# A kernel ordered by tables of planned times: retuned tables, tables of their own for the first steps, two key buffers, and first query loads issued by ScalarE

## The chip, the cores and the metric

The kernel runs on one core of a Trainium2 chip. The metric is the device time of one execution in microseconds. Before the change it is 1298.58 us, the median of three runs (1295.53 to 1300.79). The profiled execution has a span of 1298.1 us and a mean granted TensorE clock of 0.963. The engines are PE (TensorE, with PEld for its weight loads), DVE (VectorE), ACT (ScalarE), POOL (GpSimd) and SP (SyncE, which here only issues transfers).

## The reference

```python
# q, k, v: 8 batches, 8 heads, 576 rows, 64 columns, float32
scores = np.matmul(q, k.transpose(0, 1, 3, 2)) / np.sqrt(64)
kth = np.partition(scores, -32, axis=-1)[..., -32:-31]   # 32nd largest of each row
scores = np.where(scores >= kth, scores, -1e9)
attn = softmax(scores)                                    # over the kept entries
x = (attn @ v) regrouped as (4608 tokens, 512)
h = x @ w_in                                              # 512 x 1024
solu = h * softmax(h)
ln = (solu - mean(solu)) / sqrt(var(solu) + 1e-6) * g_ln
return ln @ w_out                                         # 1024 x 512
```

The weights arrive as 64-bit numbers and are turned into float32 on the chip, in 16 chunks of 128 by 512 (8 of `w_in`, 8 of `w_out`).

## The kernel before, in words

All the work is in `fast_path`. After it one number, `bad`, tells whether some row was not handled by the fast method; only then a general path would run, and with these inputs it does not.

**The attention is cut into 32 steps**, four for each of the eight batches. A step handles nine query tiles of 128 rows against 576 keys: two head pairs, two chunks of 128 rows of each head, and one tile that gathers the last 64 rows of two heads. For a step `i` the functions run as follows; the letter is the engine.

- Keys: `load_k` (SP, L653 to L665, one 256 KB transfer and two small ones for the last 64 rows of queries and keys), `load_v` (L667), `prep_t` and `prep_k` (PE transposes, L695 and L708), `prep_tc` and `prep_kc` (ACT copies, L701 and L718), `moments` (PE, L729) and `moments_c` (ACT, L735). There is one head pair's worth of these per step.
- Queries: `load_q` (SP, L739 to L751: four transfers of 64 KB and two of 16 KB), `prep_q` (PE transposes), `prep_qc` (ACT copy to `qT`, L769).
- A first guess of each row's threshold: `spread` (PE, `y_ps` L780), `spread_v` (DVE, `yq` L798), `spread_r` (DVE, L809), `first_p` (POOL, square root and scaling, L814 to L820), `first` (DVE, L828).
- Scores: `scores` (PE, `s_ps` L858, two tiles at a time) and `evac` (ACT, copy to `X`, L867, one for each of nine tiles).
- Thresholds made better by counting: `count0` (DVE, L875), `second` (DVE, L886), `count1` (seven by ACT, L897, and two by DVE, L875), `third` (DVE, L909), `count2` (ACT, `sg` L932), `side` (DVE, `al` L941). Then `nearest` and `best` (DVE, L953 and L960) find the eight scores nearest to the threshold, and `count_off` (ACT) and `kth` (DVE) choose the exact 32nd largest among them.
- Softmax: `exps` (ACT, L968), `keep` (DVE, mask and sum, L997), `inverse` (DVE, L1005), `norm` (POOL, L1012).
- Output: `transpose_p` (PE, `tp_p` L1026) and `copy_p` (ACT, `PT` L1038), `transpose_last` (PE, L1056) and `copy_last` (ACT, L1064) for the last 64 columns, `attn_v` (PE, `om` L1075) and `copy_v` (ACT, `xTm` L1087), each once for either head pair.

**The second block is cut into 36 token tiles** of 128 tokens. A tile runs through `mm1` (PE, `h_ps` L1099, two halves of four matmuls each), `hexp` (ACT), `solu` (DVE), `square` (ACT), `ln` (POOL), `transpose_ln` (PE) and `copy_ln` (ACT), `mm2` (PE, `o_ps` L1157, two halves) and `store` (ACT copy to `osb` L1164 and a transfer). Its first matmul reads `xTm`, which two steps together fill: so tile `t` of batch `b` is placed two steps after that batch's step `t`.

**The weight chunks**: `load_w` (SP), `w_bits` (DVE, `w_tmp`, L589 to L597), `w_low` (ACT, L605), `w_mul` and `w_add` (POOL), `w_gain` (POOL). At the end each chunk is loaded once more and its range tested: `w_again`, `w_exp`, `w_check`.

**The order is written out by hand.** Every call of such a function gets a planned time from a table; the list of calls is sorted by it and emitted in that order, and this fixes the queue of instructions of PE, ACT, DVE and POOL. An engine takes its queue strictly in order and waits where an operand is not ready. The transfers that SP issues follow in the order of their calls.

```python
    for i in range(NSTEP):
        all_times(i * STEP, step_times, i)
    for n in range(len(pairs)):
        for f, times in key_times:
            at(n // NP * NP * STEP + times[n % NP], f, n)
...
    with tc.manual_schedule(engines={E.PE, E.Activation, E.DVE, E.Pool}):
        for _, _, f, args in sorted(todo, key=lambda x: x[:2]):
            f(*args)
```

`STEP` is 39, and times are only places in the order. `step_times` holds one place for each call of a step and is the same for all 32 steps; `key_times` has four places for each call, one for each head pair of a batch; `first_times` serves the token tiles of batch 0, `token_times` the later ones, `tails_times` and `last_times` the tiles of left-over rows and those after the last step; `weights_times` has absolute places.

**Buffers** come from pools: `p1` has one buffer for each name, `p2` two, `p4` four, `p8` eight. `km`, the keys as loaded, is in `p1`: the next `load_k` waits until PE has read the last one in `prep_k` and `moments`. `qm` is in `p1` too. In PSUM there are three pools of two buffers each: `ps_big` for scores, `y_ps` and `h_ps`; `ps_tp` for transposes; `ps_o` for `om`, `o_ps` and `pre`, the product of `prep_t` and `moments`.

Of the kernel before, what the change touches and what calls it, by code (L numbers as in the profile page):

```python
# [15 lines left out]
P = 128  # L16
# [427 lines left out]
def fast_path(  # L444
# [23 lines left out]

    nc = tc.nc
# [30 lines left out]

    pairs = [(b, hp) for b in range(B) for hp in range(NP)]
    steps = []
    for b in range(B):
        for half in range(2):
            for n in range(NP // 2):
                two = (2 * n + half, 2 * n + 1 - half)
                chunks = [(hp, 2 * half + t) for hp in two for t in range(2)]
                steps.append((b, chunks, two[0]))
# [144 lines left out]
    def load_k(n):  # L653
# [4 lines left out]
        d["k"] = p1.tile([P, 2 * NM, D], F32, tag="km", name="km")  # L658
# [80 lines left out]
    def load_q(i):  # L739
        b, chunks, x = steps[i]  # L740
        d = st[i]
        d["q"] = p1.tile([P, NT, D], F32, tag="qm", name="qm")
        for c, (hp, t) in enumerate(chunks):
            nc.sync.dma_start(
# [5 lines left out]
        for h in range(2):  # L750
            nc.sync.dma_start(  # L751
                out=d["q"][h * ST : (h + 1) * ST, 2 * NM, :], in_=q[b, 2 * x + h, SM:S, :]
            )

    def keys_of(i, c):

        b, chunks, x = steps[i]
        return ks[NP * b + (x if c == NM else chunks[c][0])]
# [217 lines left out]
    def kth(i):  # L976
# [3 lines left out]
        hot = small.tile([P, NT, 8], F32, tag="hot", name="hot")  # L980
# [84 lines left out]

    def attn_v(i, part):
        o = st[i]["om", part] = ps_o.tile([P, 512], F32, tag="o", name="om")
        n = 2 * P if part else SP
        vm, vt = keys_of(i, 2 * part)["v"]
        pt = pt_of(i, part)[:, :, 0:n]  # L1070

        for c in range(NM + 1):
            for h in range(2):
                hd = slice(h * ST, (h + 1) * ST)
                nc.tensor.matmul(  # L1075
                    out=o[h * D : (h + 1) * D, 0:n],
                    lhsT=vm[:, h, c, :] if c < NM else vt[hd, :],
                    rhs=pt[:, h * NM + c, :] if c < NM else pt[hd, 2 * NM, :],
                    start=(c == 0), stop=(c == NM),
                )  # L1080

    def copy_v(i, part):
        b, chunks, x = steps[i]
        hp, t = chunks[2 * part]
        o = st[i]["om", part]
        m = once(xs, ("m", b, t // 2), lambda: p2.tile([P, NP, 2 * P], F32, tag="xTm", name="xTm"))
# [256 lines left out]
    for f, needed, chunks, times in weights_times:  # L1343
        for n, time in zip(chunks, times):
            if needed:
                at(time, f, n)
# [105 lines left out]
```

## Time and profile before

| what | value |
|---|---|
| time, median of three runs | 1298.58 us (1295.53 to 1300.79) |
| profiled span | 1298.1 us |
| PE busy | 1194.8 us, 92%, 6243 matmuls |
| DVE busy | 1154.8 us, 89%, 2974 instructions |
| ACT busy | 1118.8 us, 86%, 2446 instructions |
| POOL busy | 479.6 us, 37%, 583 instructions |
| costliest group of PE | `o_ps` L1157, 576 matmuls, 261.8 us |
| costliest group of DVE | `junkv` L875, 288 counts of 801 ns, 230.7 us |
| costliest group of ACT | `sg` L932, 256 counts of 768 ns, 195.6 us |
| bytes moved | 57.00 MB, mean 44 GB/s |

Three engines are busy for most of the time, so the sums over the whole span do not say which of them holds up the end: that has to be read stage by stage. The profile has a view for this, which gives each engine's busy time in chosen stretches, and one that lists, for each engine, which instruction of it waited for which instruction of another, how long in all, how often, and how long at most. A third one follows the chain of work that ended last back to the start and adds up its parts by engine.

### The profile page before, as it was taken

The page shows a single profiled execution, that of the slowest core. Times are in us where ns is not written, and L with a number is a line of the kernel's source. Part 1 is how long each engine was busy: PE and PEld are TensorE (multiplying, and loading weights), DVE is VectorE, ACT ScalarE, POOL GpSimd, SP SyncE. Part 2 cuts the span into 40 slices and gives each one's busy share as a digit, 9 for nine tenths or more (in the row PEclk, how much of TensorE's full clock was granted, in tenths as well). Part 3 has the DMA queues.
Part 4 walks back from the last instruction along what each step waited for, and adds up shares of the span by engine and source line. Part 5 has one row for each costly group of instructions (what it writes and reads, how often), then busy time and mean ns, then how long its engine had stood idle before and what let it go on. Part 6 is the DMA issues. An engine that isn't in the chain of part 4 may idle for free.

```text
span 1298.1 us, 20306 instructions
## 1 busy us (share of the span) xinstructions
PE 1194.8 (92%) x6243; PEld 658.0 (51%) x6243; DVE 1154.8 (89%) x2974; ACT 1118.8 (86%) x2446; POOL 479.6 (37%) x583
## 2 busy tenths in 40 slices
PE   5645879999999999999999999999999999998996
PEld 3323445555555555555555555555555555554543
DVE  4899999999999997999999997999999997999612
ACT  3787889999999889999999889999999889999534
POOL 4244654443333234443333244443333234443310
PEclk9666889999999999999999999999999999999999
DMA  6212211101110111101210112111210111102421
GB/s 163 81 43 61 67 38 28 37 22 37 46 36 17 30 32 50 34 23 31 54 36 18 30 30 54 28 29 30 55 35 19 31 28 43 30 9 73 130 73 44
DMA packets 106246, 57.00 MB, mean 44 GB/s; under 512 B 89224, under 2 KB 97424, under 8 KB 106128
## 3 DMA queue, kind: packets, MB, share of 16 engines
q1 hardware_dynamic: 106128, 55.61, 15.7%
q8 instruction: 52, 0.85, 0.3%
q14 instruction: 66, 0.54, 0.1%
HBM read 46.14 MB, written 9.44 MB: 43 GB/s over the span
## 4 chain that ended last, share of the span: by engine, by line
PE 59%; ACT 18%; DVE 15%; issue 3%; POOL 3%; DMA 1%; SPq 0%; DVEq 0%; POOLq 0%; ACTq 0%
PE o_ps L1157 15%; PE s_ps L858 12%; PE h_ps L1099 12%; PE tp_p L1026 7%; PE om L1075 7%; DVE junkv L875 4%; ACT junka L897 4%; DVE E L997 3%; ACT sg L932 3%; ACT PT L1038 2%; PE tp_ln L1146 2%; ACT E L968 2%; DVE w L953 2%; DVE w L960 2%; ACT X L867 2%
## 5 line engine op out<-in xcount | busy, mean ns | idle before, releaser
L1157 PE MATMUL o_ps<-w_out,lnT 128*128 128x512 f32 x576 | 261.8, 598 | 0.2 <-ACT osb L1164 0.2
L875 DVE TENSOR_SCALAR_CACHE_REDUCE junkv<-X,t 128x576 bf16<-128x576 f32 x288 | 230.7, 801 | 11.9 <-ACT X L867 7.3
L1012 POOL TENSOR_SCALAR E<-E,rden 128x576 f32<-128x576 f32 x256 | 204.7, 813 | 87.0 <-DVE rden L1008 76.5
L925 POOL TENSOR_SCALAR tt<-t 128x9 f32<-128x9 f32 x32 | 21.8, 680 | 573.3 <-DVE t L919 573.3
L1099 PE MATMUL h_ps<-w_in,xTm 128*128 128x512 f32 x512 | 226.7, 595 | 0.3 <-ACT xTm L1087 0.3
L953 DVE SCALAR_TENSOR_TENSOR w<-X,al,sg 128x576 f32<-128x576 f32 x256 | 210.6, 824 | 0.1
L960 DVE MAX8 w<-w 128x8 f32<-128x576 f32 x288 | 210.5, 749 | 0.0
L997 DVE SCALAR_TENSOR_TENSOR E<-X,kth,E 128x576 f32<-128x576 f32 x256 | 200.0, 818 | 9.7 <-ACT E L968 9.6
L858 PE MATMUL s_ps<-kT,qT 64*128 64x288 f32 x1024 | 195.7, 458 | 5.5 <-ACT X L867 4.5
L932 ACT ACTIVATE sg<-X,t 128x576 bf16<-128x576 f32 x256 | 195.6, 768 | 2.8 <-DVE t L919 2.8
L897 ACT ACTIVATE junka<-X,t 128x576 bf16<-128x576 f32 x224 | 174.3, 778 | 19.4 <-DVE t L888 15.6
L867 ACT ACTIVATE X<-s_ps 128x576 f32<-128x576 f32 x256 | 157.2, 655 | 36.0 <-PE s_ps L858 32.4
L1026 PE MATMUL tp_p<-ident,E 128*128 128x128 f32 x1024 | 155.5, 285 | 26.4 <-POOL E L1012 21.6
L1026 PEld LDWEIGHTS tp_p<-ident,E 128*128 128x128 f32 x1024 | 116.0, 144 | 92.9 <-issue 37.5
L1038 ACT COPY PT<-tp_p 128x512 f32<-128x512 f32 x256 | 145.6, 595 | 19.5 <-PE tp_p L1026 19.3
L1157 PEld LDWEIGHTS o_ps<-w_out,lnT 128*128 128x128 f32 x576 | 104.3, 190 | 110.6 <-issue 107.8
L1099 PEld LDWEIGHTS h_ps<-w_in,xTm 128*128 128x128 f32 x512 | 94.6, 190 | 109.7 <-issue 102.4
L968 ACT ACTIVATE E<-X 128x1152 f32<-128x1152 f32 x128 | 146.5, 1174 | 0.0
L1075 PE MATMUL om<-PT,vm 128*64 128x256 f32 (+1 forms) x1024 | 140.0, 416 | 0.0
L858 PEld LDWEIGHTS s_ps<-kT,qT 64*128 64x128 f32 x1024 | 116.2, 199 | 46.7 <-ACT X L867 18.1
L1075 PEld LDWEIGHTS om<-PT,vm 128*64 128x64 f32 x1024 | 68.5, 138 | 59.7 <-issue 22.5
L818 POOL TENSOR_TENSOR zs<-zs,phalf 128x9 f32<-128x9 f32 x32 | 70.2, 2194 | 2.7
(127 smaller groups left out, 1631.8 us busy)
## 6 DMA issues: line engine op xcount, KB each, us to landing
km<-in_k_dram SPq DMA_DIRECT2D x32, 256.0 KB, 3.3
qm<-in_q_dram SPq DMA_DIRECT2D x128, 64.0 KB, 2.1
vm<-in_v_dram SPq DMA_DIRECT2D x32, 256.0 KB, 2.8
out_dram<-osb SPq DMA_DIRECT2D x32, 256.0 KB, 2.3
w_raw<-in_moe_w_in_dram SPq DMA_DIRECT2D x8, 512.0 KB, 4.4
w_raw<-in_moe_w_out_dram SPq DMA_DIRECT2D x8, 512.0 KB, 3.3
w_again<-in_moe_w_in_dram SPq DMA_DIRECT2D x8, 512.0 KB, 4.6
w_again<-in_moe_w_out_dram SPq DMA_DIRECT2D x8, 512.0 KB, 4.1
```

Source lines behind the costliest of these rows:

```text
L858: nc.tensor.matmul(out=s[:, half, 0:SH], lhsT=queries_of(i, t)[hd, :], rhs=kT[hd, k0 : k0 + SH], start=True, stop=True,)
L875: nc.vector.tensor_scalar(out=junk, in0=x_of(i, j), scalar1=st[i][t][:, j : j + 1], scalar2=None, op0=ALU.is_ge, op1=ALU.add, accum_out=co ...
L897: nc.scalar.activation(out=junk, in_=x_of(i, j), func=AF.Sign, scale=-1.0, bias=d["t1"][:, j : j + 1], accum_out=columns(i, "n1")[:, j : j ...
L932: nc.scalar.activation(out=d["sg", j], in_=x_of(i, j), func=AF.Sign, scale=-(1.0 + 2.0**-23), bias=d["t2"][:, j : j + 1], accum_out=column ...
L953: nc.vector.scalar_tensor_tensor(out=w, in0=x_of(i, j), scalar=d["al"][:, j : j + 1], in1=d.pop(("sg", j)), op0=ALU.subtract, op1=ALU.mult,)
L960: nc.vector.max(w8[:, j, :], st[i].pop(("w", j)))
L997: nc.vector.scalar_tensor_tensor(out=e, in0=x_of(i, j), scalar=d["kth"][:, j : j + 1], in1=e, op0=ALU.is_ge, op1=ALU.mult, accum_out=den_a ...
L1012: nc.gpsimd.tensor_scalar(out=e, in0=e, scalar1=st[i]["rden"][:, j : j + 1], scalar2=1.0, op0=ALU.mult, op1=ALU.mult,)
L1026: nc.tensor.transpose(tp[:, c, :], e[:, c * P : (c + 1) * P], ident)
L1075: nc.tensor.matmul(out=o[h * D : (h + 1) * D, 0:n], lhsT=vm[:, h, c, :] if c < NM else vt[hd, :], rhs=pt[:, h * NM + c, :] if c < NM else ...
L1099: nc.tensor.matmul(out=h[:, half, :], lhsT=x[:, c, :], rhs=w_in[:, c, half * 512 : (half + 1) * 512], start=(c == 0), stop=(c == NP - 1),)
L1157: nc.tensor.matmul(out=o, lhsT=d["lnT"][:, c, :], rhs=w_out[:, c, :], start=(c == 0), stop=(c == NF - 1),)
```

## The change

The instructions are the same as before, with the same operands and counts, apart from the engine that issues six loads. What is changed is where they stand:

- The steps 0 to 3 get tables of places of their own (`early_times`), since at the start the engines have other work beside the steps (loads, decoding of weights) than later. `key_times` has separate places for the first batch.
- All other tables are given new places, those of the steady steps and of the token tiles too. The places of the last range test of the weights are now counted from the end of the last step.
- `km` moves to `p2`: two key loads can be under way or in use at once.
- The six query loads of step 0 are issued by ScalarE, so that SyncE can issue other loads in that time.
- `hot`, a small operand of `kth`, moves to `p1` and has one buffer instead of three.
- The list of steps is written in another form; it gives the same four steps of a batch in the same order. `runs_of` is a helper for steps whose two chunks belong to different head pairs; there is none, so it returns one run each time.

```diff
--- before.py
+++ after.py
...
     pairs = [(b, hp) for b in range(B) for hp in range(NP)]
     steps = []
     for b in range(B):
-        for half in range(2):
-            for n in range(NP // 2):
-                two = (2 * n + half, 2 * n + 1 - half)
-                chunks = [(hp, 2 * half + t) for hp in two for t in range(2)]
-                steps.append((b, chunks, two[0]))
+        for t in range(NM):
+            two = (t % 2 * 2 + t // 2, t % 2 * 2 + 1 - t // 2)
+            steps.append((b, [(hp, t // 2 * 2 + n) for hp in two for n in range(2)]))
     NSTEP = len(steps)
...
         d = ks[n]
 
-        d["k"] = p1.tile([P, 2 * NM, D], F32, tag="km", name="km")
+        d["k"] = p2.tile([P, 2 * NM, D], F32, tag="km", name="km")
         nc.sync.dma_start(
...
     def load_q(i):
-        b, chunks, x = steps[i]
+        b, chunks = steps[i]
         d = st[i]
         d["q"] = p1.tile([P, NT, D], F32, tag="qm", name="qm")
+        eng = nc.scalar if i == 0 else nc.sync
         for c, (hp, t) in enumerate(chunks):
-            nc.sync.dma_start(
+            eng.dma_start(
                 out=d["q"][:, 2 * c : 2 * c + 2, :],
                 in_=q[b, 2 * hp : 2 * hp + 2, 0:SM, :].rearrange("h (p t) d -> p t h d", t=NM)[
                     :, t, :, :
                 ],
             )
         for h in range(2):
-            nc.sync.dma_start(
-                out=d["q"][h * ST : (h + 1) * ST, 2 * NM, :], in_=q[b, 2 * x + h, SM:S, :]
+            eng.dma_start(
+                out=d["q"][h * ST : (h + 1) * ST, 2 * NM, :], in_=q[b, 2 * chunks[1][0] + h, SM:S, :]
...
-        hot = small.tile([P, NT, 8], F32, tag="hot", name="hot")
+        hot = p1.tile([P, NT, 8], F32, tag="hot", name="hot")
...
+    def runs_of(i, part):
+
+        chunks = steps[i][1]
+        n, end = 2 * part, SP if part == 0 else 2 * P
+        if chunks[n][0] == chunks[n + 1][0]:
+            return [(n, slice(0, end))]
+        return [(n, slice(0, P)), (n + 1, slice(P, end))]
...
+        for n, cols in runs_of(i, part):
+            vm, vt = keys_of(i, n)["v"]
+            pt = pt_of(i, part)[:, :, cols]
+            for c in range(NM + 1):
+                for h in range(2):
+                    hd = slice(h * ST, (h + 1) * ST)
+                    nc.tensor.matmul(
+                        out=o[h * D : (h + 1) * D, cols],
+                        lhsT=vm[:, h, c, :] if c < NM else vt[hd, :],
+                        rhs=pt[:, h * NM + c, :] if c < NM else pt[hd, 2 * NM, :],
+                        start=(c == 0), stop=(c == NM),
+                    )
...
+        for n, cols in runs_of(i, part):
+            hp, t = chunks[n]
+            w = min(cols.stop, 2 * P) - cols.start
+            nc.scalar.copy(
+                out=m[:, hp, t % 2 * P : t % 2 * P + w], in_=o[:, cols.start : cols.start + w]
+            )
...
     step_times = [
-        (load_q, [()], [-52.3]),
-        (prep_q, [()], [-25.66]),
-        (prep_qc, [()], [-21.32]),
-        (spread, [()], [-14.74]),
-        (spread_v, [()], [-12.28]),
-        (spread_r, [()], [-9.11]),
-        (first_p, [()], [-5.94]),
-        (first, [()], [-3.94]),
-        (scores, range(5), [-7.74, -5.46, -3.54, 0.79, 4.68]),
-        (evac, range(9), [-4.99, -4.94, -2.71, -2.43, -0.91, -0.66, 1.75, 4.87, 8.58]),
-        (count0, range(9), [-3.49, -3.39, -1.8, -1.65, 1.1, 2.22, 6.88, 7.72, 8.66]),
-        (count1, range(9), [13.91, 15.21, 12.34, 15.17, 15.19, 16.89, 17.13, 16.96, 21.1]),
-        (count2, range(9), [29.61, 24.17, 28.68, 23.34, 23.78, 23.94, 47.62, 27.29, 29.63]),
-        (second, [()], [11]),
-        (third, [()], [22.2]),
-        (exps, range(5), [52.85, 51.89, 50.14, 56.99, 57.42]),
-        (side, range(3), [37.21, 28.03, 49.2]),
-        (inverse, range(3), [62.57, 64.96, 71.31]),
-        (count_off, [()], [50.83]),
-        (kth, [()], [59.45]),
-        (nearest, range(9), [41.07, 47.51, 39.3, 32.69, 29.76, 32.16, 57.74, 55.76, 51.21]),
-        (best, range(9), [46.43, 52.3, 45.06, 36.45, 31.16, 33.82, 59.19, 58.14, 52.97]),
-        (keep, range(9), [60.36, 61.34, 60.51, 62.49, 61.26, 61.16, 68.47, 62.8, 65.92]),
-        (norm, range(9), [66.71, 64.69, 67.66, 72.59, 68.38, 72.61, 76.63, 77.78, 82.81]),
+        (load_q, [()], [-58.55]),
+        (prep_q, [()], [-26.85]),
+        (prep_qc, [()], [-21.44]),
+        (spread, [()], [-11.91]),
+        (spread_v, [()], [-10.17]),
+        (spread_r, [()], [-9.05]),
+        (first_p, [()], [-6.37]),
+        (first, [()], [-3.36]),
+        (scores, range(5), [-6.57, -4.23, -1.67, -0.1, 3.03]),
+        (evac, range(9), [-6.03, -5.64, -3.74, -3.55, -0.01, 0.68, 2.22, 9.73, 12.17]),
+        (count0, range(9), [-2.25, -3.2, -1.07, 2.59, 8.49, 10.7, 5.36, 13.44, 15.33]),
+        (count1, range(9), [19.53, 20.34, 18.01, 18.92, 20.31, 19.41, 19.38, 22.97, 21.96]),
+        (count2, range(9), [30.97, 30.7, 31.03, 25.59, 24.99, 26.9, 48.53, 28.62, 43.23]),
+        (second, [()], [16.81]),
+        (third, [()], [23.22]),
+        (exps, range(5), [53.23, 54.01, 52.33, 52.15, 62.57]),
+        (side, range(3), [37.33, 28.25, 50.1]),
+        (inverse, range(3), [60.99, 67.16, 72.66]),
+        (count_off, [()], [48.75]),
+        (kth, [()], [58.31]),
+        (nearest, range(9), [47.26, 49.52, 40.75, 35.17, 33, 34.35, 52.94, 54.93, 51.94]),
+        (best, range(9), [48.46, 51.34, 42.82, 35.72, 34.06, 35.92, 56.52, 55.91, 53.4]),
+        (keep, range(9), [60.14, 59.06, 60.26, 64.48, 65.54, 61.16, 63.66, 67.49, 66.79]),
+        (norm, range(9), [66.27, 61.28, 63.28, 72.57, 68.19, 72.62, 74.13, 79.22, 81.91]),
         (transpose_p, range(9), [
-            70.08, 67.75, 72.27, 74.68, 72.98, 77.69, 79.24, 81.24, 83.57,
+            68.02, 65.33, 72.11, 76.54, 74.05, 76.91, 79.08, 79.54, 83.19,
         ]),
-        (copy_p, range(8), [71.1, 70.74, 73.88, 77.75, 75.87, 78.46, 81.22, 82.02]),
-        (copy_pt, [()], [84.44]),
-        (transpose_last, range(2), [85.94, 86.48]),
-        (copy_last, range(2), [87.65, 89.55]),
-        (attn_v, range(2), [87.9, 90.3]),
-        (copy_v, range(2), [90.37, 92.29]),
+        (copy_p, range(8), [71.22, 70.67, 73.74, 79.54, 77.27, 80.21, 81.58, 82.52]),
+        (copy_pt, [()], [84.09]),
+        (transpose_last, range(2), [84.07, 85.15]),
+        (copy_last, range(2), [84.49, 87.91]),
+        (attn_v, range(2), [89.05, 89.32]),
+        (copy_v, range(2), [92.23, 94.22]),
     ]
 
+    early_times = [
+        [
+            (load_q, [()], [-101.52]),
+            (prep_q, [()], [-40.19]),
+            (prep_qc, [()], [-25.81]),
+            (spread, [()], [-24.43]),
+            (spread_v, [()], [-21.5]),
+            (spread_r, [()], [-19.87]),
+            (first_p, [()], [-19.82]),
+            (first, [()], [-4.41]),
+            (scores, range(5), [-23.82, -19.21, -3.2, 4.15, 5.64]),
+            (evac, range(9), [-9.69, -8, -2.34, -0.97, -0.82, 1.71, 5.12, 5.4, 12.24]),
+            (count0, range(9), [-4.21, 6.95, -0.12, 8.37, 9.25, 13.58, 14.66, 14.73, 16.17]),
...
+        [
+            (load_q, [()], [-45.59]),
+            (prep_q, [()], [-31.03]),
+            (prep_qc, [()], [-24.5]),
+            (spread, [()], [-18.19]),
+            (spread_v, [()], [-16.17]),
+            (spread_r, [()], [-13.83]),
+            (first_p, [()], [-5.28]),
+            (first, [()], [-2.65]),
+            (scores, range(5), [-17.7, -6.49, -3.84, 3.96, 7.4]),
+            (evac, range(9), [-10.98, -15.47, -5.47, -3.9, -2, 3.26, 4.92, 5.05, 9.29]),
+            (count0, range(9), [4.79, 4.01, -0.33, 2.87, 8.67, 5.95, 8.5, 7.49, 10.25]),
+            (count1, range(9), [20.71, 23.7, 15.09, 18.62, 21.19, 18.32, 12.42, 21.75, 12.27]),
+            (count2, range(9), [32.02, 29.66, 34.27, 25.25, 27.92, 25.64, 34.1, 33.72, 28.55]),
+            (second, [()], [10.74]),
...
     key_times = [
-        (load_k, [-71.77, -54.35, -34.54, -26.23]),
-        (load_v, [46.71, 33.98, 89.74, 55.28]),
-        (prep_t, [-50.7, -40.81, -7.18, 29.61]),
-        (prep_tc, [-44.69, -33.63, -1.87, 33.99]),
-        (prep_k, [-57.81, -29.05, -14.02, 12.97]),
-        (prep_kc, [-52.21, -21.98, -13.67, 19.04]),
-        (moments, [-60.64, -32.24, -4.08, 14.96]),
-        (moments_c, [-42.18, -31.04, 2.87, 15.92]),
+        (load_k, [-128.19, -71.8, -42.03, -28.02], [-75.42, -73.58, -72.11, -1.78]),
+        (load_v, [38.78, 46.1, 53.1, 40.37], [50.34, 47.97, 37.98, 26.9]),
+        (prep_t, [-60.08, -49.19, -18.13, 29.56], [-64.45, -58.18, -24.06, 20.73]),
+        (prep_tc, [-41.94, -38.55, 3.19, 34.96], [-62.19, -48.03, -8.09, 28.01]),
+        (prep_k, [-55.9, -54.46, -37.69, -20.18], [-60.75, -29.27, -14.5, 22.89]),
+        (prep_kc, [-31.78, -29.07, 9.4, 4.48], [-52.34, -18.85, -13.66, 26.15]),
+        (moments, [-56.79, -48.19, -23.98, 11.28], [-61.35, -32.7, -8.19, 21.34]),
+        (moments_c, [-41.65, -28.87, 7.59, 17.57], [-55.84, -31.58, 3.7, 25.58]),
     ]
 
...
     token_times = [
-        (mm1, range(2), [55.81, 54.67]),
-        (hexp, [()], [62.36]),
-        (solu, [()], [64.42]),
-        (square, [()], [64.52]),
-        (ln, [()], [70.28]),
-        (transpose_ln, range(2), [71.2, 73.87]),
-        (copy_ln, range(2), [73.54, 76.75]),
-        (mm2, range(2), [104.76, 108.8]),
-        (store, [()], [120.44]),
+        (mm1, range(2), [56.06, 57.63]),
+        (hexp, [()], [60.42]),
+        (solu, [()], [64.02]),
+        (square, [()], [66.27]),
+        (ln, [()], [67.97]),
+        (transpose_ln, range(2), [71.79, 75.48]),
+        (copy_ln, range(2), [73.59, 77.3]),
+        (mm2, range(2), [103.81, 108.4]),
+        (store, [()], [124.81]),
     ]
...
     weights_times = [
         (load_w, True, range(NW), [
-            -179.04, -126.3, -52.39, -38.25, -33.45, 2.48, 8.22, 5.52, 52.89, 51.11, 62.18,
-            83.53, 63.6, 105.69, 111.2, 108.65,
+            -200.79, -75.24, -62.59, -31.18, -23.75, -6.2, 22.36, 37.34, 43.22, 55.77, 75.55,
+            85.44, 89.7, 93.75, 120.97, 113.35,
         ]),
         (w_bits, w_wide, range(NW), [
-            -155, -52.03, -42.38, -5.42, 15.63, 19.48, 57.75, 77.84, 84.56, 85.78, 92.26,
-            104.44, 115.57, 124.08, 129.87, 135.07,
+            -162.34, -72.58, -39.71, -16.17, 17.63, 22.92, 28.06, 81.13, 88.01, 91.7, 95.09,
+            114.48, 108.39, 125.73, 132.18, 130.95,
         ]),
         (w_low, w_wide, range(NW), [
-            -109.8, -76.02, -28.31, 1.47, 11.32, 38.79, 64.91, 76.6, 83.01, 89.83, 92.36,
-            105.31, 118.79, 123.48, 128.94, 132.88,
+            -161.61, -66.91, -24.98, 2.3, 10.34, 36.86, 42.62, 74.86, 82.2, 90.49, 93.64,
+            117.06, 119.45, 125.96, 132.2, 135.71,
         ]),
...
+    at_end = (w_again, w_exp, w_check)
+
+    at(-250.76, load_g)
     for f, needed, chunks, times in weights_times:
         for n, time in zip(chunks, times):
             if needed:
-                at(time, f, n)
+                at(time + (NSTEP * STEP if f in at_end else 0.0), f, n)
...
     for i in range(NSTEP):
-        all_times(i * STEP, step_times, i)
+        all_times(i * STEP, early_times[i] if i < len(early_times) else step_times, i)
     for n in range(len(pairs)):
-        for f, times in key_times:
-            at(n // NP * NP * STEP + times[n % NP], f, n)
+        for f, first, later in key_times:
+            at(n // NP * NP * STEP + (later if n >= NP else first)[n % NP], f, n)
...
```

## The prediction

> **What bounds the kernel now.** I read the stages first, then who waits for whom in them, then the chain. A table of stages (us, busy time of PE, PEld, DVE, ACT, POOL, granted clock, DMA share, GB/s):
>
> ```profile
> 0.00:80.00 80.00, 38.49 (x181) 23.97 (x182) 56.06 (x139) 49.23 (x111) 24.33 (x41) 0.77 0.38 99
> 80.00:200.00 120.00, 88.59 (x490) 51.57 (x489) 117.61 (x267) 91.97 (x203) 65.73 (x67) 0.79 0.20 59
> 200.00:400.00 200.00, 193.92 (x1060) 108.31 (x1060) 194.58 (x516) 190.97 (x418) 80.75 (x97) 1.00 0.13 33
> 400.00:1180.00 780.00, 771.54 (x4141) 424.01 (x4138) 732.94 (x1920) 724.30 (x1583) 280.48 (x345) 1.00 0.12 32
> 1222.00:1298.00 76.00, 64.75 (x228) 31.50 (x226) 13.88 (x40) 30.76 (x68) 11.00 (x16) 0.96 0.22 73
> 302.50:595.30 292.80, 289.59 (x1562) 159.85 (x1561) 275.02 (x723) 273.16 (x601) 106.68 (x131) 1.00 0.13 34
> ```
>
> There are three regimes. From 200 us on PE is full: the last row is one period of eight steps, PE 289.59 of 292.80 (98.9%), DVE 275.02 (94%). So a step costs 36.6 us, of which PE works 36.2 and idles 0.4. Before 200 us PE is idle for 72.9 us, and from 80 to 200 DVE is the bound (117.61 of 120). From 0 to 80 no engine is full: DVE idles 23.9 us. Last, the 66 us from the end of the attention to the end of the last token tile are PE's again. The end is therefore: when the first steps let PE fill up, plus PE's remaining work, plus its small idles. Who keeps DVE waiting in 0 to 80 (us in total, times, longest), and below, who keeps PE in 0 to 240:
>
> ```profile
> DVE w_tmp L589 <- DMA w_raw<-in_moe_w_in_dram: 11.0, 2, 5.8
> DVE junkv L875 <- ACT X L867: 4.7, 5, 1.3
> DVE yq L798 <- PE y_ps L780: 1.7, 2, 1.0
> DVE step L909 <- ACT junka L897: 1.3, 1, 1.3
> DVE t L828 <- POOL zs L818: 1.3, 1, 1.3
> DVE junkv L875 <- ACT Xt L867: 1.2, 1, 1.2
> DVE al L941 <- ACT sg L932: 0.8, 1, 0.8
> ```
>
> ```profile
> PE y_ps L780 <- ACT qT L769: 28.1, 6, 10.4
> PE tp_p L1026 <- POOL E L1012: 19.1, 5, 7.2
> ```
>
> The two 5-us waits of DVE are for the first weight chunks, and behind the second of them stands the first `yq`. PE's waits of up to 10.4 us are no loss of their own: what stands behind them needs DVE's later work of the step. The chain says the same of the whole: PE 59%, DVE only 15%.
>
> ```profile
> PE 59%; ACT 18%; DVE 15%; issue 3%; POOL 3%; DMA 1%; SPq 0%; DVEq 0%; POOLq 0%; ACTq 0%
> ```
>
> **What the Trainium skill says.** "DMA: Bandwidth & Descriptors", Issuing engines are not separate DMA queues: transfers started by different engines run on the same 16 DMA engines, and a second issuer saves only the time to issue. No transfer is issued by ACT in this trace, so it is not shown; but the first six query loads hold SyncE from 4.27 to 8.44 us, and this is what the edit takes from it. "TensorE: Matmul & The Clock Gate", Part 1: a PE that is not kept busy is clocked at half rate. The trace agrees: clock 0.54 from 40 to 80 us, where PE is busy 16.7 of 40, and 1.00 from 200 on. So early matmuls are slow because PE has little to do, not the reverse. "Perfetto Trace Analysis", Optimization Strategy: find the gaps on the engine that matters in the regime of interest and what releases it. Here that is DVE until about 200 us and PE after.
>
> **The change, part by part.**
>
> Nothing computed changes. The four head pairs and chunks of each step come out the same from the new formula, `runs_of` returns one run each time, so `attn_v` and `copy_v` issue the same 20 matmuls and 3 copies; `hot` with one buffer is used by DVE alone, in order. These cost 0.
>
> *Start.* Before, SyncE issues two weight chunks, key 0, and six query loads; the second key's load goes out at 9.49 us, after PE has transposed key 0 out of the only buffer. Its tail lands near 13.1 (PE `pre` starts at 13.13 on it), the query transposes follow at 15.43, `qT` at 17.17, `y_ps` at 17.81, `yq` at 18.44. After, by the order of issue: one weight chunk, key 0 and its tails, one weight chunk, key 1 without a wait. ACT issues the six query loads, but behind its first `w_low`, which waits for chunk 0 (5.20 us before; about 4 with one chunk ahead). At the 0.5 to 0.7 us an issue that SyncE shows, they go out from 4.7 to 8: as early as before, no earlier. What stands behind them on ACT is `w_low` of chunk 1 and the copies of key 0, which PE has not made before 8 us: hidden. Key 1: issue near 4.2, landing near 9 (a key load takes 3.4 us at least, 5.9 behind 1 MB). Its tails wait for PE's `prep_t` of key 0, near 7, and land near 10. Then copies on ACT, `qT` near 13.5. But PE has key 2's transposes ahead of `y_ps`, and that load is issued near 10, behind a value load and weight chunk 2: landing 14 to 15.5, so `y_ps` 15 to 16.5. DVE has chunk 2 ahead of `yq` as before. Gain of `yq`: 1.3 to 2.8 us; I take 2. From `yq` to the end of the first counts (36.1) the order is the same, paced by scores and evacuations of 3.05 us a pair: nothing more.
>
> *36 to 60 us.* ACT now makes `qT` of step 1 before the seven `count1` of step 0, not after; so `y_ps` of step 1 no longer waits until 43.46, and DVE has `spread_v` (1.05) and two weight chunks (1.55 each) ahead of `third` beside two counts: 5.9 us of work against ACT's 7 x 0.90 = 6.3, so it waits 0.4 where it waited 1.26. The waits of 0.96 for `y_ps` and about half of 0.83 for the first signs go too, and part of the 0.9 for evacuations after that, as these now stand between the signs. Together 2.5 us less, of which I count 2.
>
> *60 to 200 us.* Adding DVE's durations along both orders, the work ahead of the first `inverse` of step 2 is 141.5 us in each, of step 3 179.2 in each: no work is moved past what PE waits for. DVE idles only 2.4 us here before: nothing to gain. `mm1` of the first tile waits longer for its copies (13 us of ACT work stand between `copy_last` and the last `copy_v` of step 1, 7 before), but behind it PE then waits 7.2 us for POOL anyway (162.9 to 170.1): hidden. So the start gives 2 + 2 = 4 us, bounds 1 and 8.
>
> *Steady steps.* PE's work is the same and 98.9% full, so a new order can win at most 0.4 us x 28 = 11 us and can lose more. One place I can price. PE runs `attn_v` (3.0 + 2.5 us), `prep_q` 0.5, then `mm1`, whose third matmul (0.86 later) needs the last copy of `xTm` on every second step. Before, that copy ended as it was needed:
>
> ```profile
> 295.84 2.37 PE L1075 MATMUL om<-PT,vm 128*64 128x320 f32 x16
> 296.56 0.42 ACT L1064 COPY PT<-tp_pt 128x320 f32<-128x320 f32 x1
> 302.37 4.03 PE L1099 MATMUL h_ps<-w_in,xTm 128*128 128x512 f32 x9
> 302.37 0.39 ACT L1087 COPY xTm<-om 128x256 f32<-128x256 f32 x1
> ```
>
> After, ACT has between `copy_last` and that copy: a store 0.46, a `count2` 0.76, two `evac` 0.55 each, `count_off` 0.2, `copy_last` 0.25, four `exps` 1.06 each, a copy 0.36: 7.4 us, and 0.4 for the copy itself: it ends 7.5 to 7.8 us after PE starts `attn_v` (ACT is less late at `copy_last` now). PE needs it at 3.0 + 2.5 + 0.5 + 0.86 = 6.8, or 7.1 to 7.5 where a `prep_t` lies between or the last head is read fourth. Wait 0 to 0.95 on every second step, 2.2 us in eight, 7 us over 28. Against it: ACT may come to `copy_last` earlier than I think, and DVE has 1.1 us less work ahead from step 4 on. POOL's `ln` stands one `norm` earlier and PE finds its results ready by a margin of about 1 us. I take +1.5, ends -5 and +12.
>
> *Tail.* The same tiles on PE, one `mm1` ahead of an `mm2`; checks on ACT as many: 0, within 1.5.
>
> Sum: 1298.6 - 4 + 1.5 = 1296.
>
> **Rivals.**
> - B, the start frees more: `y_ps` at 15, evacuations better laid (7 us), and the retuned steps lose none of PE's time and win 3.5 of 11: 1288. For it: 23.9 us of DVE idle, three quarters of it named above. Against: half is the wait for the first transfers, which still have 2.5 MB to bring.
> - C, a wait takes its place: the late copies cost the full 7 and the narrower margins on POOL another 3, the start gives only 3: 1305.5, slower. For it: a PE with no slack, and the sum above. Against: half a microsecond of error in ACT's lag undoes it.
> - D, nothing: transfers bound the start (0.5 MB of weights and a value load before key 2), no steady change: 1298.6.
>
> **How the numbers follow.** Forecast 0.40, B 0.32, C 0.20, D 0.08. Faster by over 0.5% is under 1292.1: most of B (0.29) and the low end of the forecast (0.06), 0.35. Slower is over 1305.1: half of C and a little of the forecast's high end, 0.15. The rest 0.50. Range: the bounds of the forecast are 1298.6 - 8 - 5 and 1298.6 - 1 + 12, 1286 to 1310; reached down for most of B and cut above where only the end of C lies: 1283 to 1307.
>
> **What would show it.** Right: `yq` starts at 15.5 to 17 us; DVE idle in 0 to 80 near 20; the first `tp_p` of step 2 near 166 (170.14 before); a period of eight steps of 292.5 to 294, with new waits of PE `h_ps` on ACT `xTm` up to 1 us. Wrong: if `yq` is not earlier, the start gives nothing; if a period is under 291 or over 295, the steady steps decided, and my margin for ACT was mis-sized; if the first `mm1` delays PE past the first `tp_p` of step 2, the early tables cost.

## The result and the profile after

The changed kernel takes 1315.95 us, the median of four runs (1313.72 to 1317.51); the kernel before takes 1299.04 (1295.53 to 1300.79). The ratio is 1.0132, with a 95% interval of 1.0106 to 1.0158: slower by 17 us. The prediction was 1296.

The stages of the changed kernel, with the same columns as before, and below them one period of eight steps, from the last output copy of step 8 to that of step 16. The period of the kernel before, cut in the same way, stands in the second fence.

```profile
0.00:80.00 80.00, 45.45 (x206) 26.50 (x208) 62.50 (x155) 55.26 (x126) 30.81 (x47) 0.71 0.42 113
80.00:200.00 120.00, 88.68 (x493) 49.62 (x491) 114.39 (x281) 94.79 (x209) 66.20 (x67) 0.85 0.18 52
200.00:400.00 200.00, 193.88 (x1072) 107.28 (x1071) 190.04 (x493) 187.32 (x406) 76.08 (x92) 1.00 0.13 33
402.40:703.30 300.90, 292.74 (x1565) 160.65 (x1560) 273.55 (x728) 274.85 (x600) 106.59 (x131) 0.99 0.13 33
```

```profile
408.00:700.60 292.60, 289.40 (x1562) 159.60 (x1561) 275.83 (x725) 273.25 (x600) 106.66 (x131) 1.00 0.13 34
```

Read them in two directions. In the first 80 us DVE now works 62.5 us where it worked 56.1, so it idles 17.5 instead of 23.9: the start is better. But a period has grown from 292.6 to 300.9 us. PE's idle time in it grew from 3.2 to 8.2 us, and its busy time by 3.3 although its work is the same. Of this, 1.7 us are a short stretch at half clock, seen below. The other 1.6 are a lasting cost of the new order: the later runs with the new steady places, in which those waits are gone, still show PE 291.1 to 291.3 us busy in a period, against 289.4. Why the same matmuls take longer there was not looked into.

Where the difference stands along the run can be read from the last output copy (`xTm`) of each step: it comes 7.7 us earlier in step 3 (224.4 against 232.1), 5.6 earlier in step 8, 2.7 later in step 16 and 12.2 later in step 31. So the start gives 7.7 us, the steady steps take 19.9, and the end takes another 4.1: 16.3 in all, the difference of the two profiled spans (1314.4 and 1298.1). The 7.7 is one profile's: in five profiles of kernels with the same tables for the first steps (the changed one and four of the runs below) that copy of step 3 comes at 222.3 to 227.2 us, 4.9 to 9.8 earlier than before.

What PE waits for in the steady steps, in the same sixteen steps, is the view that names the loss. First the kernel before, then the changed one (us in total, times, longest):

```profile
PE tp_pt L1060 <- ACT PT L1041: 2.4, 10, 0.2
PE pre L729 <- ACT kT L702: 1.4, 4, 0.3
PE tp_ln L1146 <- ACT PT L1038: 1.1, 2, 0.6
```

```profile
PE tp_ln L1160 <- ACT PT L1039: 5.9, 6, 1.4
PE pre L729 <- ACT kT L702: 5.0, 4, 1.2
PE o_ps L1171 <- ACT mom L735: 2.1, 2, 1.0
PE tp_pt L1061 <- ACT PT L1042: 1.9, 8, 0.2
```

Three waits have grown or are new, and none of them is `h_ps` on `xTm`, the one that the prediction priced. The second is `moments` waiting for `prep_tc`. In time, on PE of the changed kernel:

```profile
400.58 0.27 PE L695 MATMUL pre<-ident,qt 64*128 64x64 f32 x1
400.69 0.22 PE L695 MATMUL pre<-ident,kt 64*128 64x64 f32 x1
402.16 0.32 PE L729 MATMUL pre<-km 128*64 128x64 bf16 x8 [1.25 <-ACT kT L702]
402.41 5.40 PE L1113 MATMUL h_ps<-w_in,xTm 128*128 128x512 f32 x8
```

`prep_t` writes columns 0 to 127 of the PSUM tile `pre`, `prep_tc` (ACT) copies these out, and `moments` writes columns 128 to 191 of the same tile. No data pass between `moments` and `prep_tc`; what they share is the tile. The new key places put the three in this order, directly behind each other, for the first key of a batch. So PE stands for 1.25 us until ACT has read. This wait is seen five times from 400 us on, and after the first of them PE's clock was granted at half rate for 3.4 us: the eight `h_ps` took 5.40 us, where they took 3.70 after each of the other four, as here:

```profile
559.75 0.32 PE L729 MATMUL pre<-km 128*64 128x64 bf16 x8 [1.25 <-ACT kT L702]
560.00 3.70 PE L1113 MATMUL h_ps<-w_in,xTm 128*128 128x512 f32 x8
```

The first wait in the list is the same fault in the other direction, for the third key. Here `moments` is placed just ahead of `prep_tc`, so ACT stands until PE comes to it:

```profile
462.52 0.32 PE L729 MATMUL pre<-km 128*64 128x64 bf16 x8
462.76 1.24 PE L859 MATMUL s_ps<-kT,qT 64*128 64x288 f32 x8
462.88 0.27 ACT L701 COPY kT<-pre 128x128 f32<-128x128 f32 x1 [1.12 <-PE pre L729]
...
464.67 1.06 ACT L1039 COPY PT<-tp_p 128x512 f32<-128x512 f32 x2
465.39 0.63 PE L1160 MATMUL tp_ln<-ident,solu 128*128 128x128 f32 x4 [1.39 <-ACT PT L1039]
```

ACT loses 1.12 us, two counts and then the copies of `tp_p` follow 1.12 us late, and the next `transpose_ln`, which needs the buffer that the first copy frees, keeps PE waiting for 1.39 us. That an ACT wait comes back as a PE wait 2.5 us later is read here, and was then tested.

### The profile page after: what moved, and what is told of

Its sections match the earlier page's. It is cut to its first block, busy times and chain, and to the rows that moved or that the text cites. A ratio compares the mean times of both kernels' runs of the same rounds, so it can differ in the third digit from the quotient of the medians.

```text
span 1314.4 us, 20336 instructions
## 1 busy us (share of the span) xinstructions
PE 1201.7 (91%) x6243; PEld 657.2 (50%) x6243; DVE 1144.0 (87%) x2974; ACT 1124.4 (86%) x2446; POOL 481.0 (37%) x583
## 4 chain that ended last, share of the span: by engine, by line
PE 63%; DVE 15%; ACT 15%; issue 3%; POOL 2%; DMA 1%; SPq 0%; ACTq 0%; DVEq 0%; POOLq 0%
PE o_ps L1171 15%; PE h_ps L1113 13%; PE s_ps L859 13%; PE tp_p L1027 9%; PE om L1084 7%; DVE junkv L876 4%; ACT E L969 3%; ACT sg L933 3%; DVE w L961 3%; ACT junka L898 3%; DVE w L954 3%; PE tp_ln L1160 2%; DVE E L998 2%; PE tp_qk L708 2%; ACT X L868 1%
## 5 line engine op out<-in xcount | busy, mean ns | idle before, releaser
L1013 POOL TENSOR_SCALAR E<-E,rden 128x576 f32<-128x576 f32 x256 | 210.2, 833 | 540.8 <-DVE rden L1009 458.6
L1113 PE MATMUL h_ps<-w_in,xTm 128*128 128x512 f32 x512 | 230.5, 600 | 1.4 <-ACT xTm L1099 1.4
L859 PE MATMUL s_ps<-kT,qT 64*128 64x288 f32 x1024 | 200.7, 454 | 17.8 <-DVE mean L802 10.3
L954 DVE SCALAR_TENSOR_TENSOR w<-X,al,sg 128x576 f32<-128x576 f32 x256 | 213.9, 845 | 0.1
L898 ACT ACTIVATE junka<-X,t 128x576 bf16<-128x576 f32 x224 | 175.2, 782 | 10.1 <-DVE t L889 4.3
L1027 PE MATMUL tp_p<-ident,E 128*128 128x128 f32 x1024 | 153.9, 283 | 19.3 <-POOL E L1013 11.6
L819 POOL TENSOR_TENSOR zs<-zs,phalf 128x9 f32<-128x9 f32 x32 | 67.5, 2109 | 2.7
L1124 ACT ACTIVATE e_sb<-h_ps 128x1024 f32<-128x1024 f32 x36 | 36.4, 1011 | 34.0 <-PE h_ps L1113 33.7
```

Of the source, the lines that this page charges most:

```text
L859: nc.tensor.matmul(out=s[:, half, 0:SH], lhsT=queries_of(i, t)[hd, :], rhs=kT[hd, k0 : k0 + SH], start=True, stop=True,)
L898: nc.scalar.activation(out=junk, in_=x_of(i, j), func=AF.Sign, scale=-1.0, bias=d["t1"][:, j : j + 1], accum_out=columns(i, "n1")[:, j : j ...
L954: nc.vector.scalar_tensor_tensor(out=w, in0=x_of(i, j), scalar=d["al"][:, j : j + 1], in1=d.pop(("sg", j)), op0=ALU.subtract, op1=ALU.mult,)
L1013: nc.gpsimd.tensor_scalar(out=e, in0=e, scalar1=st[i]["rden"][:, j : j + 1], scalar2=1.0, op0=ALU.mult, op1=ALU.mult,)
L1027: nc.tensor.transpose(tp[:, c, :], e[:, c * P : (c + 1) * P], ident)
L1113: nc.tensor.matmul(out=h[:, half, :], lhsT=x[:, c, :], rhs=w_in[:, c, half * 512 : (half + 1) * 512], start=(c == 0), stop=(c == NP - 1),)
```

## The experiments

**The steady places or the start?** Four runs split the change. In the first, the tables of the steady steps and of the end are those of before; in the second, the tables of the start and of the end.

```diff
     step_times = [
-        (load_q, [()], [-58.55]),
+        (load_q, [()], [-52.3]),
...
     key_times = [
...
-        (moments, [-56.79, -48.19, -23.98, 11.28], [-61.35, -32.7, -8.19, 21.34]),
+        (moments, [-56.79, -48.19, -23.98, 11.28], [-60.64, -32.24, -4.08, 14.96]),
...
+            at(n // NP * NP * STEP + (seam[f] if n == 7 else places[n % NP]), f, n)
```

> The changed kernel with the tables of the first steps, first keys, first tiles and weight chunks kept, and those of the steady steps and of the end taken back from the kernel before (the fourth key of the second batch has places of its own, so that the two sets of tables fit together). Theory P, the start wins and the new steady places lose: the last output copy of step 3 was 7.7 us earlier after the change, and from there the old places keep that lead: 1299.0 - 7.7 = 1291, period of eight steps 292.6. Rival Q, the new start leaves the engines in a phase that makes the later steps slower: the period stays near 300 and the time near 1312. Rival R, a step paced by PE gives the lead back: 1299.

Measured: 1302.68 us, ratio 1.0023 (1.0013 to 1.0033). The lead was 7.5 us at step 1 (7.9 in the changed kernel), and was lost within steps 2 and 3, where places of the two sets meet: 3.4 behind at step 3. From there the period is 292.7, and to step 31 only 1.2 us more are lost. So theory P is right on the period, since the old places cost nothing beside the new start, and wrong on the total: 11 us are lost where the two sets of tables meet. That they do not fit each other is read from the place of the loss; it was not tested. This run also keeps the rest of the change (the rewritten loops, one buffer for `hot`, two for `km`), so none of that is what lengthens the period.

The second run keeps only the steady places:

```diff
     early_times = [
-            (load_q, [()], [-101.52]),
+            (load_q, [()], [-52.3]),
...
     key_times = [
...
-        (moments, [-56.79, -48.19, -23.98, 11.28], [-61.35, -32.7, -8.19, 21.34]),
+        (moments, [-60.64, -32.24, -4.08, 14.96], [-61.35, -32.7, -8.19, 21.34]),
...
-        eng = nc.scalar if i == 0 else nc.sync
+        eng = nc.sync
```

> The changed kernel with the start's tables and the end's taken back from the kernel before and the first query loads on SyncE again: only the places of the steady steps, of the steady key preparation and of the steady token tiles are new, and km has two buffers. Theory P: the loss of steps 4 to 31, 19.9 us (from 7.7 ahead to 12.2 behind), appears alone: 1299.0 + 19.9 = 1319, period of eight steps 299 to 301. Rival Q, the start makes it: 1299.

Measured: 1334.46 us, ratio 1.0271 (1.0251 to 1.0291). Here too the tables do not fit where they meet: 15.8 us are lost by step 3. From step 3 to step 31 another 22.3 go, where P expected 19.9, and the period is 301.0. So the loss belongs to the steady places, whatever the start.

**The end.** The last tiles and the last range tests at their old places:

```diff
...
         (w_check, w_wide, range(NW), [
-            139.45, 100.14, 52.19, 75.33, 162.62, 70.41, 115.86, 92.42, 203.61, 215.17, 193.04,
-            232.31, 119.3, 174.72, 202.39, 195.53,
+            92.79, 97.85, 29.65, 84.62, 123.59, 53.74, 118.88, 79.12, 168.86, 196.15, 122.39, 245.58, 184.99, 171.36, 169.83, 185.70,
...
```

> The changed kernel with the places of the last tiles and of the last range test of the weights taken back from the kernel before. Theory P: after the last output copy of the last tile the changed kernel takes 13.7 us to the end, the kernel before 9.6, as two more range tests and five more sums stand behind it: 1316.0 - 4.1 = 1311.9. Rival Q, the end waits for the last stores anyway: 1316.

Measured: 1313.84 us, ratio 1.0107 (1.0087 to 1.0127): 2.1 us less than the changed kernel (3.3 by the ratios, which set each against runs of the kernel before taken at the same time), where 4.1 was expected; the intervals overlap. In the traces, from the last output copy to the last comparison (`bad`) it takes 3.7 us in the changed kernel, 1.6 in this run and in the kernel before. The rest of the 4.1 lies behind all work: from there to the end of the span the profiles show 8.0 us (before), 9.0 (this run) and 10.1 (changed), and 9.3 and 6.5 in two later runs with this same end. So about 2 us are the order's, and the rest differs from run to run.

**The two waits.** In the changed kernel `moments` of the first and third key goes ahead of `prep_t`, two numbers:

```diff
-        (moments, [-56.79, -48.19, -23.98, 11.28], [-61.35, -32.7, -8.19, 21.34]),
+        (moments, [-56.79, -48.19, -23.98, 11.28], [-64.6, -32.7, -24.3, 21.34]),
```

> The changed kernel with moments of the first and third key of each later batch placed just ahead of prep_t instead of behind it. PE then has no matmul into pre that follows ACT's copy out of pre (wait 1.25 us once a batch), and ACT's copy no longer waits 1.1 us for moments with three counts and the copies behind it, on which PE waits 1.39 us once a batch. Theory P, these two waits on PE are most of the steady loss: 7 x (1.25 + 1.39) = 18.5 us less, 1316.0 - 18.5 = 1297.5, and no less than 1302 if half of the second wait comes from elsewhere; period near 294. Rival S, PE's waits are only where a slower ACT or DVE shows, and move elsewhere: 1314 to 1317.

Measured: 1298.16 us, ratio 0.999 (0.9979 to 1.0). That is 17.8 us less (18.5 by the ratios), where P said 18.5. P's sum took each wait seven times; the changed kernel's trace has five of 1.25 us and six of 1.39, and 1.7 us of half clock, 16.3 in all, and the two profiled spans differ by 16.0. So the cause is P's, and that its number fits so closely is in part luck. Both waits are gone from PE's list of the sixteen steps:

```profile
PE o_ps L1171 <- ACT mom L735: 2.5, 2, 1.3
PE tp_pt L1061 <- ACT PT L1042: 1.9, 8, 0.2
PE tp_p L1027 <- POOL E L1013: 0.5, 2, 0.3
```

The rival, that the waits move elsewhere, falls. A third way, a tile of its own for `moments`, was not tried. To size the two apart, only the first key was moved:

```diff
-        (moments, [-56.79, -48.19, -23.98, 11.28], [-61.35, -32.7, -8.19, 21.34]),
+        (moments, [-56.79, -48.19, -23.98, 11.28], [-64.6, -32.7, -8.19, 21.34]),
```

> The changed kernel with moments of the first key of each later batch moved ahead of prep_t, that of the third key left where the change has it. Theory P, each misplaced key costs by itself: 7 x 1.25 = 8.8 us less than 1316.0, and up to 1.7 more where PE's clock fell once behind that wait: 1305.5 to 1307.5; the wait of PE for ACT's late copies behind the third key, 1.39 us once a batch, stays. Rival S, the two are one delay that only moves from key to key: 1298 or 1316.

Measured: 1307.0 us, ratio 1.0061 (1.0043 to 1.008): 9.0 us for the first key, so 8.8 for the third (9.2 each by the ratios). In its trace the `transpose_ln` waits of 1.39 us stand, one in each of six batches, and the `moments` waits are gone. The second, indirect wait costs as much as the direct one.

**Is it enough by itself?** The kernel before, with only the first key's order as the change has it:

```diff
-        (prep_tc, [-44.69, -33.63, -1.87, 33.99]),
+        (prep_tc, [-50.55, -33.63, -1.87, 33.99]),
...
-        (moments, [-60.64, -32.24, -4.08, 14.96]),
+        (moments, [-50.4, -32.24, -4.08, 14.96]),
```

> The kernel before, in which for the first key of each batch prep_tc and moments are placed right behind prep_t, as the change has them, and nothing else is moved. Theory P: PE waits for ACT's copy out of pre once a batch, 1.25 us or more, with nothing to do beside it: 1300.5 + 7 x 1.25 = 1309, from 1307 to 1314 if ACT is later there. Rival S, PE has as much slack elsewhere and wins it back: 1300.5.

Measured: 1318.22 us, ratio 1.015 (1.013 to 1.0171): 18.3 us slower, twice what P expected. The direction is P's, the size is not: here ACT comes to `prep_tc` much later in every second batch.

```profile
PE pre L729 <- ACT kT L702: 10.4, 8, 4.0
```

The trace shows waits of 3.0 us (once) and 4.0 (twice) in three of the six batches from 280 us on, 0.5 in the others, and a small second one of 0.34 in each: 14.5 us in all, of which the last kind, 2.0, stands in the kernel before too. Behind the two longest PE ran at half clock for 6.8 and 3.4 us. The profiled run was one of the quicker (1315.62 us); its last output copy of step 31 is 15.2 us late. Two moved numbers in a table slow the old kernel by as much as the whole change did.

**What the start's gain is made of.** One buffer for `km` again, in the version with both `moments` moved:

```diff
-        d["k"] = p2.tile([P, 2 * NM, D], F32, tag="km", name="km")
+        d["k"] = p1.tile([P, 2 * NM, D], F32, tag="km", name="km")
```

> The changed kernel with moments moved, and one buffer for km as before. Theory A, the second buffer is needed at the start alone: the second key load waits until PE has read the first, near 8 us instead of 4.7, and yq comes 2 to 4 us later: 1300 to 1302. Rival B, the start is bound by DVE's later work: 1298. Rival C, with the three key loads of a batch planned close together, one buffer makes SyncE or PE wait in the steady steps too: 1305 or more.

Measured: 1304.55 us, ratio 1.0038 (1.0024 to 1.0052): 6.4 us more. `yq` comes at 21.6 us instead of 17.3, PE waits longer for key loads in the first 240 us, and the last output copy is 3.7 us later than with two buffers in step 3, 4.7 in step 4 and 6.0 in step 31. So the second buffer is needed at the start above all (A), and is worth more than A said; 1.3 us go in the later steps. The run takes away more than a buffer: SyncE's transfers do not strictly follow the order of the calls (in the kernel before, the first query loads, called behind the second key load, go out ahead of it, at 4.27 and 9.49 us), and with one buffer the first 48 of them come in another order, the second key (9.62 us, 4.67 with two buffers) behind two value loads. The 6.4 us are the buffer with the order that follows from it. PE's waits for key loads from 0 to 240 us, first with one buffer, then with two:

```profile
PE tp_qk L708 <- DMA km<-in_k_dram: 7.9, 3, 5.3
```

```profile
PE tp_qk L708 <- DMA km<-in_k_dram: 2.0, 1, 2.0
```

The first query loads were given back to SyncE:

```diff
-        eng = nc.scalar if i == 0 else nc.sync
+        eng = nc.sync
```

> The changed kernel with moments moved, and the first query loads issued by SyncE again. In the trace ACT spends 6.3 us on the six issues (6.5 to 12.8 us, 1.05 us each, where SyncE took 4.2 for them before) and ACT's copies of key 0 come at 13.4 though PE made them at 7.1. Theory A, these issues hold up the start as much as they free SyncE: 1297 to 1299, first yq within 1 us of 17.3. Rival B, freeing SyncE is what brings yq 1.5 us forward: yq at 18.5 to 20 and 1299.5 to 1301.

Measured: 1297.93 us, ratio 0.9983 (0.9974 to 0.9993), against 0.999 (0.9979 to 1.0) with ScalarE: no difference. `yq` comes 1.2 us later (18.5), and the end does not feel it. The trace with ScalarE shows what is paid for the earlier `yq`: ACT issues from 6.48 to 12.80 us and its copies of the first key stand behind that. The 1.05 us each of the expectation is a mean that includes pauses: the rows below merge several issues, and one issue alone takes 0.37 to 0.80 us, as on SyncE (0.47 to 0.60), with pauses of up to 1.9 us between them. What the pauses wait for, the trace does not show.

```profile
6.48 4.40 ACTq L745 DMA_DIRECT2D qm<-in_q_dram  x4
11.41 1.39 ACTq L752 DMA_DIRECT2D qm<-in_q_dram  x2
13.41 0.25 ACT L701 COPY kT<-pre 128x128 f32<-128x128 f32 x1
```

**A version that beats both.** Both `moments` moved, the old end, and `moments_c` of the first key ahead of the counts, since PE waited for it twice (1.26 us each) in the list above:

```diff
-        (moments_c, [-41.65, -28.87, 7.59, 17.57], [-55.84, -31.58, 3.7, 25.58]),
+        (moments_c, [-41.65, -28.87, 7.59, 17.57], [-60.4, -31.58, 3.7, 25.58]),
```

> The changed kernel with moments moved as in the run before, moments_c of the first key of each later batch moved ahead of the seven counts it stood behind on ACT (PE waited 1.26 us for it at 563 and 857 us), and the end's places taken back. Theory P, the losses add up: 1298.2 - 2.5 - 2.1 (what the end gave alone) = 1293.5, between 1291 and 1295. Rival: the end's places fit another phase and give nothing, 1296; or the copy, moved, delays the copies of xTm and gives nothing, 1298.

Measured: 1295.02 us, ratio 0.9969 (0.9961 to 0.9978), faster than both kernels; P's sum, 1293.5, gave 1.5 us more. The period of eight steps is 293.2 us, still not under the 292.6 of before: PE idles 2.0 us in it where it idled 3.2, but is busy for 291.3 where it was for 289.4. What this version wins, it wins at the start: its last output copy is 9.8 us ahead of before in step 3 and 7.2 in step 31, so steps paced by PE do not give the lead back (rival R of the first run). A last run on top of it had the queries issued by SyncE behind the second key:

```diff
-            (load_q, [()], [-101.52]),
+            (load_q, [()], [-71.7]),
...
-        eng = nc.scalar if i == 0 else nc.sync
+        eng = nc.sync
```

> The version with both moments moved, moments_c moved and the old end, in which the first query loads are issued by SyncE behind the second key's loads, so that neither ACT's copies of key 0 (13.4 us) nor the second key load (4.7) wait for them. Theory A, ACT's copies were what the first yq waited for: yq at 15 to 16 and 1293. Rival B, the queries themselves then come late, behind the tails that wait for PE: yq at 17.5 or later and 1295 or more.

Measured: 1294.34 us, ratio 0.9965 (0.9949 to 0.998). Rival B's `yq` (19.3 us, 1.8 later), and no loss by it: the two cannot be told apart. Within 2 us, the first `yq` is not what sets the end.

## Why the prediction was wrong

- **What bounds the kernel**: right. From 200 us on each small stop of PE was paid in full: the stops and the half clock that went with the two moved `moments` add up to 16.3 us in the trace, and the time fell by 17.8. At the start, 1 to 2 us of the first `yq` meant nothing.
- **Steady steps**: this step failed. It took "+1.5, ends -5 and +12" from one place, the late copies of `xTm`. PE waits for it once in the whole run, 1.4 us, at 148 us. The steady loss was 19.9 us, and 16.3 of it came from a place that the prediction put at nothing: the order of `prep_t`, `prep_tc` and `moments` around the shared tile `pre`. The table of the keys was in the diff, with `moments` 3.1 units behind `prep_t` for the first key and 0.1 ahead of `prep_tc` for the third; the list of waits of before had the very row (`pre` L729 on `kT` L702, 2.5 us in seven), small because the old places kept the three apart. The prediction does not mention it. Its sign for this case, a period over 295, came true, but the reason that it gave there, its margin for ACT, is not the one. "PE's work is the same" failed too, in small: the same matmuls take 1.6 to 1.9 us longer in eight steps of the new order. Rival C had the right kind of cause, a wait on a PE without slack, and the right sign, but the wrong wait and too small a size (1305.5).
- **Start**: the direction was right and the size too small. Forecast were 2 us up to `yq` and 2 from 36 to 60 us, all of it less idle time of DVE. Here are DVE's busy times in 0 to 40 and 40 to 60, before and after:

```profile
0.00:40.00 40.00, 20.86 (x46) 0.99 0.62 161
40.00:60.00 20.00, 15.57 (x40) 0.50 0.23 61
```

```profile
0.00:40.00 40.00, 24.43 (x59) 0.92 0.70 183
40.00:60.00 20.00, 18.41 (x43) 0.50 0.24 70
```

  DVE idles 3.6 us less in the first and 2.8 less in the second. But the five profiles with this start have 17.5 to 20.1 us of DVE idle in 0 to 80, and near 20 was forecast: this term was about right. `yq` starts at 16.9 (forecast 15.5 to 17, taken gain 2, measured 1.6). The first `tp_p` of step 2 comes at 159.9, where 166 was forecast. The DVE work that it stands behind ends with the first `inverse` of that step, 9.8 us earlier than before (158.6 against 168.4). Of these, 4.3 are less idle time, and 5.5 are a term that the prediction put at nothing: it added DVE's durations to "141.5 us in each" order, and the same work (329 and 330 instructions) took 142.7 us before and 137.2 after. The three profiles with the old start have 142.2 to 143.0, the nine with the new start 135.5 to 137.7. A DVE instruction has no fixed duration here. The same one, in the kernel before, first alone and then with POOL at work beside it:

```profile
6.39 0.43 DVE L597 TENSOR_SCALAR w_tmp<-w_tmp 128x512 uint32<-128x512 uint32 x1
8.35 1.59 POOL L632 TENSOR_TENSOR w_in<-w_tmp,w_low 128x512 f32<-128x512 f32 x1
8.86 1.37 DVE L597 TENSOR_SCALAR w_tmp<-w_tmp 128x512 uint32<-128x512 uint32 x1
```

  Up to that `inverse`, all 22 DVE instructions that took over 0.2 us more than the shortest of their kind had POOL working beside them, and all 21 in the changed kernel. That the new order lets the two meet less is read from this, not tested. Nor were the early tables tested without the second key buffer, which is worth 6.4 us of the whole time with the order of transfers that it brings.
- **ACT issues the query loads**: that these are "hidden" was wrong in the detail. The length of an issue was forecast well (0.5 to 0.7; 0.37 to 0.61 in the changed kernel), but ACT came to the first at 6.2 us and not 4.7, and the pauses between them held it until 12.3, and so the copies of key 0 until 12.9. It was right for the time. What the prediction took from the Trainium skill ("DMA: Bandwidth & Descriptors", Issuing engines are not separate DMA queues), that a second issuer saves only the time to issue, agrees with the runs: with ACT the second key load goes out at 4.67 us and with SyncE at 8.05, and the times are 1298.16 and 1297.93 us.
- **Tail**: "0, within 1.5" was wrong. Two more range tests and all the final sums stood behind the last copy: 2 us of order, and about 2 that vary.
- **The range** was 1283 to 1307, and 1316 lies above it. Its upper end came from one suspected wait and a margin on POOL, and not from the number of order changes on PE that had not been looked at.
- Three small figures are off and change nothing: 2.2 us in eight steps make 7.7 over 28 and not 7; the waits of DVE that the prediction lists are 22.0 of the 23.9 us, not three quarters; and the quickest key load of the kernel before took 3.1 us, not 3.4.

## What to carry to other kernels

On an engine that is 99% busy, an order that is retuned can hardly win and can lose by every place where a producer and its consumer come to stand directly behind each other: list all such pairs that the new order brings together, also the cheap ones, and price each by its wait times its number. The wait to take is the time until the other engine, in its own order, comes to its part: it was 1.25 us in the changed kernel and up to 4.0 in the kernel before with the same order. Two writers of one PSUM tile with a reader between them are such a pair, in both directions, even where they touch different columns. And a table of places is tuned as a whole: the new start joined to the old steady tables lost 11 us where they met.

## What the runs showed of the hardware

- One issue of a query load took 0.37 to 0.80 us on ACT and 0.47 to 0.60 on SyncE. But six of them took 6.3 us from first to last on ACT, with pauses of up to 1.9 us, and 4.2 on SyncE.
- One stop of PE of 1.25 us was followed by 3.4 us at half clock in one of five cases in the changed kernel; the other four, at the same place in the order, were followed by none. In the run with the old end none of the five was. So a stop this short can cost the clock; what decides it, these traces do not show.
- A DVE instruction that takes 0.43 us alone took 1.37 beside a POOL instruction. In the first 168 us of the kernel before such lengthening adds up to 14.7 us beside POOL and to 1.4 elsewhere (each instruction against the shortest of its kind); in the changed kernel, up to the same point of the work, to 10.1 and 1.2.
